# Queries and keys by token tile, turned by DMA transposes, in a fused attention and feed-forward kernel on one core

## The chip, the cores and the metric

The kernel runs on one core of one Trainium2 chip. The metric is the device time of one execution in microseconds (us). The kernel before has a median of 168.66 us over 13 runs, between 167.62 and 169.07.

## The reference

The input x has 2048 tokens of width 448. It is normalised (mean and variance over the width, no gain or bias) to xn. Two branches read xn, and the result joins them. Inputs and output are bf16.

```python
# attention: 16 heads of 28; each token looks back at 8 positions with stride 2
qkv = (xn @ wqkv) -> q, k, v                    # wqkv is 448 x 1344
idx = pos[:, None] - 2 * arange(8)              # masked where negative
attn = softmax(q . k[idx] * 28 ** -0.5)
s = (attn . v[idx]) @ wo                        # wo is 448 x 448
# feed-forward
h = gelu(xn @ w1 + b1)                          # 448 -> 1792, tanh form
g = silu(h @ w2 + b2)                           # 1792 -> 448
out = x + s * g
```

## The kernel before

**Layout.** The tokens are reordered so that all even tokens come first and then all odd ones (`tok`, L188); a stride of two becomes a run of neighbours. There are 16 token tiles of 128 and four chunks of four tiles. The width of 448 is three full contraction tiles of 128 and a rest of 64 rows. The rest is stored twice, in both halves of the partitions, so that two 64-row matmuls can run side by side: the "tails" at L458, L480 and L513. `batch` (L413) puts two outputs' full matmuls first, then a group of tails, and then the full matmuls of two more outputs.

**Stages.** For a token tile, `stats` and `rstds` give mean and 1/deviation, and `norm` (L390) writes xn with tokens on the partitions (L393, L395). It has to be turned so that the width lies on the partitions (`xnT`): by TensorE transposes (L405) for tiles 0 to 7, and by DMA transposes on SyncE (L317) for tiles 8 to 15. `vproj` (L472) makes values with tokens on the partitions: xnT is the stationary operand and 448 columns of weights move. `qk` (L447) makes queries and keys already turned: a group of four heads, each padded from 28 to 32 rows, is the stationary operand (`wqk`, a padded copy of the raw weights `wraw`), and 256 or 512 tokens move. Chunk 0 uses 256 tokens at a time and chunks 1 to 3 use 512. The results are copied into `qT` and `kT`, one tensor for each of four head groups.

`attn` (L570) works on 17 blocks of queries: block 0 has 128 and the others 120, with 128 keys each. For a block, 16 small score products (L580) fill four PSUM banks, ScalarE takes the exponential (L586), VectorE multiplies by a mask (L594), 16 products with values (L602, called PV below) give numerator and denominator, and VectorE divides (L609, L614) into `os`. The 128 keys of a block begin at multiples of 120, so most blocks need values from two token tiles: `values` (L489) assembles them in one of six buffers `v` with two moves within SBUF. In the same way one or two moves put the 120 rows of `os` into token tiles `ot`, and a DMA transpose makes `oT`. All these moves go through `dma_sb` (L309), issued by SyncE.

`ff1` (L504) and `ff2` (L529) are the feed-forward, with GELU on ScalarE; ff2's result goes through y (L552), tanh (L558) and g (L562). `final` (L635) multiplies oT by wo (L639), then by g (L644), adds x (L649) and stores the tile from SyncE (L653).

**What sets the order.** Nothing is issued in source order. Each step is a task with an engine, a cost, dependencies, buffers that it takes and gives, and a priority. `_Plan.run` (L79) plays a list schedule over these costs, and the instructions are then emitted in the order of the planned starts. Each engine, and each queue of DMA issues, keeps that order at run time: an instruction that waits holds all behind it on its engine. The priorities stand in the table `PRIO` (L704). A move on SyncE is charged 0.55 us and a transpose 1.3 us.

```python
def dma_sb(dst, src, deps, take=(), give=()):
    def fn(k):
        nc.sync.dma_start(dst(k), src())
    a = plan.add("SP", 0.55, fn, deps, 75, take=take)
    return a, plan.add("DMA", 0.3, lambda _: None, [a], 75, give=give, tail=1.5)
```

Of the kernel before, what the change touches and what calls it, by code (L numbers as in the profile page):

```python
# [153 lines left out]
def kernel(  # L154
# [39 lines left out]
    def rows(halves, pos, n):  # L194
        h, r = divmod(pos, HALF)
        return halves[h, r:r + n, :]
# [4 lines left out]
    def sb(name, shape, dt=BF16):  # L201
        return const.tile(shape, dt, name=name)
# [13 lines left out]
    b1 = sb("b1", [P, NMT], F32)  # L216
    b2 = sb("b2", [P, D])
    xnT = sb("xnT", [P, KT, S])
    qT = [sb(f"qT{g}", [P, S]) for g in range(G)]
    v_tok = [sb(f"v_tok{t}", [P, H, 32]) for t in range(9)]  # L220
    v_tok = v_tok[8:] + v_tok[1:8] + v_tok[:8]
    kT = [sb(f"kT{g}", [P, S]) for g in range(G)]
    oT = sb("oT", [P, KT, S])
    ident = sb("ident", [P, P])
    eps_t = sb("eps_t", [P, 1], F32)
# [30 lines left out]
    def buf(pool, owner, i=0):  # L256
        return pool.bufs[owner.slots[pool][i]]
# [10 lines left out]
    def copy(e, o, i):  # L268
        if e == "ACT":
            nc.scalar.copy(o, i)  # L270
        else:
            nc.vector.tensor_copy(o, i)
# [33 lines left out]
        a = plan.add(eng, 0.45, fn, [t_on] + list(deps), prio)  # L306
        return plan.add("DMA", kb / (300.0 if prio > 93 else 350.0), lambda _: None, [a], prio, tail=1.7)

    def dma_sb(dst, src, deps, take=(), give=()):  # L309
        def fn(k):  # L310
            nc.sync.dma_start(dst(k), src())
        a = plan.add("SP", 0.55, fn, deps, 75, take=take)
        return a, plan.add("DMA", 0.3, lambda _: None, [a], 75, give=give, tail=1.5)

    def dma_T(dst, src, deps, give):
        def fn(_):
            nc.sync.dma_start_transpose(out=dst, in_=src())  # L317
        a = plan.add("SP", 1.3, fn, deps, 70)
        return plan.add("DMA", 0.6, lambda _: None, [a], 70, give=(give,), tail=1.5)

    t_x = {}

# [67 lines left out]
    def norm(t, prio):  # L390
        def f1(k):
            xn = buf(p_xn, k)
            nc.vector.tensor_scalar(xn[:, :D], x_sb[:, t, :], mv[:, t, 0:1], rstd[:, t:t + 1],  # L393
                                    op0=ALU.subtract, op1=ALU.mult)
            nc.vector.tensor_copy(xn[:, D:], xn[:, KF:D])  # L395

        a = plan.add("DVE", 0.5, f1, [t_rs[t]], prio, take=(p_xn,))
        if t >= 2 * TPC:
            t_xT[t] = dma_T(xnT[:, :, t * P:(t + 1) * P], lambda: buf(p_xn, a)[:], [a], (p_xn, a, 0))
            return  # L400

        def f2(k):
            xn, tp = buf(p_xn, a), half_bank(buf(p_b, k))
            for kt in range(KT):
                nc.tensor.transpose(tp[:, kt, :], xn[:, kt * P:(kt + 1) * P], ident[:])  # L405
        b = plan.add("PE", 0.25, f2, [a, t_ident], prio, take=(p_b,), give=((p_xn, a, 0),), tail=0.15)

        def f3(k):
            copy(k.on, xnT[:, :, t * P:(t + 1) * P], half_bank(buf(p_b, b)))
        t_xT[t] = plan.add(("DVE", "ACT"), (dve(512, 2), act(512)), f3, [b], prio, give=((p_b, b, 0),))  # L410
# [36 lines left out]
    def qk(t0, t1, g, which, prio):  # L447
        cs = slice(t0 * P, t1 * P)
        n = (t1 - t0) * P
        hs = slice(H * which + 4 * g, H * which + 4 * g + 4)  # L450
        r = slice(64 * which, 64 * which + 64)
        dst, done = (kT, t_k) if which else (qT, t_q)

        def full(ps, kt, start, stop):
            nc.tensor.matmul(ps[:, :n], wqk[:, kt, hs, :], xnT[:, kt, cs], start=start, stop=stop)  # L455

        def tail(ps, start, stop):
            nc.tensor.matmul(ps[:, :n], wqk3[r, 4 * g:4 * g + 4, :], xnT[r, 3, cs], start=start, stop=stop)  # L458

        def evac(a, own, i):  # L460
            def fn(k):
                copy(k.on, dst[g][:, cs], buf(p_b, own, i)[:, :n])
            k = plan.add(("ACT", "DVE"), (act(n), dve(n)), fn, [a], prio + 2, give=((p_b, own, i),))
            for t in range(t0, t1):
                done[(g, t)] = k
        return _Job(n, full, tail, which, [t_xT[t] for t in range(t0, t1)] + t_wqk[:3], evac, (), t_wqk[3:])

    t_v, v_at, h_at = {}, {}, {}
    t_vt = {}
# [19 lines left out]
    def values(b):  # L489

        t, r = divmod(BLK[b][2], P)
        if not r:
            t_v[b], v_at[b] = [t_vt[t]], None
            return
        a, d1 = dma_sb(lambda k: buf(p_v, k)[:P - r], lambda: v_tok[t][r:], [t_vt[t]], (p_v,))
        _, d2 = dma_sb(lambda _: buf(p_v, a)[P - r:], lambda: v_tok[t + 1][:r], [a, t_vt[t + 1]])
        t_v[b], v_at[b] = [d1, d2], (p_v, a, 0)
        v_used[t + 8].append(d1)
        v_used[t + 9].append(d2)
# [70 lines left out]
    def attn(b, prio, gate, early):  # L570
# [5 lines left out]
        def f1(k):  # L576
            for g in range(G):
                for hl in range(4):
                    r = slice(32 * hl, 32 * hl + 32)
                    nc.tensor.matmul(buf(p_b, k, hl)[:, g * nq:(g + 1) * nq], kT[g][r, k0:k0 + P],  # L580
                                     qT[g][r, q0:q0 + nq], start=True, stop=True)
        a = plan.add("PE", 0.15, f1, deps + early, prio, take=(p_b,) * 4, tail=0.15, mode=32)
        pv, exps = [], []
        for hl in range(4):
# [35 lines left out]
        while q < q0 + nq:  # L620
            t, row = divmod(q, P)
            n = min(P - row, q0 + nq - q)
            first, d = dma_sb(lambda k, t=t, row=row, n=n: buf(p_ot, ot_at.get(t, k))[row:row + n, :D],
                          lambda q=q, n=n: buf(p_os, o)[q - q0:q - q0 + n, :], [o] + t_os + [d for _, d in ot[t]],
                          () if ot[t] else (p_ot,), ((p_os, o, 0),) if q + n == q0 + nq else ())
            ot[t].append((first, d))
            ot_at[t] = ot[t][0][0]
            if row + n == P:
                t_oT[t] = dma_T(oT[:, :, t * P:(t + 1) * P], lambda t=t: buf(p_ot, ot_at[t])[:], [d for _, d in ot[t]],
                                (p_ot, ot_at[t], 0))  # L630
            q += n
        return exps
# [2 lines left out]
    def final(t, prio):  # L635
        def f1(k):
            ps = buf(p_b, k)
            for kt in range(KT):
                nc.tensor.matmul(ps[:, :D], oT[:, kt, t * P:(t + 1) * P], wo[:, kt, :],  # L639
                                 start=(kt == 0), stop=(kt == KT - 1))  # L640
        a = plan.add("PE", pe(D, KT), f1, [t_oT[t]] + t_wo + [t_f2[min(t + 1, NT - 1)]], prio, take=(p_b,), tail=0.15)

        def f2(k):
            nc.vector.scalar_tensor_tensor(out=buf(p_sg, k)[:], in0=buf(p_b, a)[:, :D], scalar=0.5,  # L644
                                           in1=buf(p_g, t_g[t])[:], op0=ALU.mult, op1=ALU.mult)
        s = plan.add("DVE", dve(D), f2, [a, t_g[t]], prio + 4, take=(p_sg,), give=((p_b, a, 0), (p_g, t_g[t], 0)))

        def f3(k):
            nc.vector.tensor_tensor(out=buf(p_o, k)[:], in0=x_sb[:, t, :], in1=buf(p_sg, s)[:], op=ALU.add)  # L649
        o = plan.add("DVE", dve(D, 2), f3, [s], prio + 4, take=(p_o,), give=((p_sg, s, 0),))  # L650

        def f4(_):
            nc.sync.dma_start(rows(o_half, t * P, P), buf(p_o, o)[:])  # L653
        plan.add("SP", 0.6, f4, [o], 50, give=((p_o, o, 0),), tail=2.0)

    for t in range(2):
        stats(t)
# [27 lines left out]
    for m, w, n, lo, hi in masks:  # L685
# [13 lines left out]
        def fn(_, m=m, w=w, n=n):  # L699
# [1 line left out]
        t_mask.append(plan.add("DVE", 0.3, fn, [t_m, t_st[3]], prio=60))  # L701


    PRIO = {"project": (77, 71, 71, 36.5),  # L704
            "attn": (922.5, 900, 875, 876),
            "ff1": (72.5, 91, 75, 75),
            "ff2": (63, 73, 3, 5),
            "final": (52.5, 36.5, 49.5, 49.5, 93.5, 82.5, 101.5, 48.5)}
    blocks_of = [[b for b, (q0, nq, _) in enumerate(BLK) if (q0 + nq - 1) // CH == c] for c in range(NCH)]
    gate = [early]  # L710

    def project(c):
        p = PRIO["project"][c]
        for t in range(c * TPC, (c + 1) * TPC):
            norm(t, 97 - 2 * t if t < TPC else p + 1)
        vs = [vproj(t, t % 2, p) for t in range(c * TPC, (c + 1) * TPC)]
        if c == 0:
            for i in range(0, len(vs), 2):
                batch(vs[i:i + 1], vs[i + 1:i + 2], 96 if i == 0 else p)
        for t0, t1 in ((0, 2), (2, 4)) if c == 0 else ((c * TPC, (c + 1) * TPC),):  # L720
            for g in (0, 2):
                batch(*[[qk(t0, t1, h, w, p) for w in range(2)] for h in (g, g + 1)], p)
        if c:
            batch(vs[:2], vs[2:], p - 0.1)
        for b in blocks_of[c]:
            values(b)

# [11 lines left out]
    for c, what in ((0, "F"), (0, "A"), (1, "A"), (1, "F"), (2, "A"), (2, "F"), (3, "A"), (3, "F")):  # L739
# [6 lines left out]
        else:  # L746
# [9 lines left out]
                project(2)  # L756
                project(3)
            for t in range(c * TPC, (c + 1) * TPC):
                ff2(t, PRIO["ff2"][c])
    for t in range(NT):  # L760
        final(t, PRIO["final"][t // 2])

    plan.run()
    with tc.manual_schedule():
# [31 lines left out]
```

The softmax here doesn't subtract the row's maximum and nothing guards it: scores larger than these inputs give would overflow.

## Time and profile before

| | |
|---|---|
| median of 13 runs | 168.66 us |
| the profiled run: its own time | 168.19 us |
| the profiled run: span | 166.2 us |
| TensorE busy | 159.0 us |
| ScalarE, VectorE busy | 110.2 and 105.0 us |
| GpSimd busy | 4.4 us |
| DMA issues on SyncE after the loads | 61 moves, 24 transposes, 16 stores |
| granted TensorE clock | 0.993 |

PE is TensorE, PEld its weight loads, DVE VectorE, ACT ScalarE, POOL GpSimd and SP SyncE; SPq is SyncE's queue of instructions. Busy time is a share of the span. A matmul's end is modelled, and neighbours overlap in the pipeline, so the mean of a group is longer than the pace of a run of them. The chain of what ended last lists pieces that follow one another in time, each with its start, its length and its line, so it gives the pace. A group line gives line, engine, operation, output and inputs, shapes, count, then busy time in us and the mean in ns, and then the idle time before the group with what ended it. DMA issues have durations for the issue alone; the transfer comes afterwards.

### The profile page before, as it was taken

What the parts mean: (1) busy time and instruction counts of PE and PEld (TensorE: products, weight loads), DVE (VectorE), ACT (ScalarE), POOL (GpSimd) and SP (SyncE); (2) the same over time, 40 slices, a digit from 0 to 9 for tenths busy, and PEclk for the clock granted to TensorE, in tenths of its full rate; (3) what the DMA queues carried; (4) which work ended last, traced back from release to release, by engine and by line L of the source; (5) the groups of instructions that cost most, each with busy time, mean ns of one, the idle gap of its engine ahead of it and who ended that gap; (6) DMA issues with size and microseconds to landing.
All of it is one profiled execution on the core that took longest, in us unless ns stands there. A gap on an engine that the chain in (4) does not pass through costs nothing.

```text
span 166.2 us, 3522 instructions
## 1 busy us (share of the span) xinstructions
PE 159.0 (96%) x1316; PEld 77.3 (47%) x1328; DVE 105.0 (63%) x278; ACT 110.2 (66%) x201; POOL 4.4 (3%) x29
## 2 busy tenths in 40 slices
PE   6999999999999999999999999999999999999980
PEld 2465535454544355434556533543466553345530
DVE  4798993097899968320296910694798987006672
ACT  3286379987888975698876798455894468851210
POOL 7300000000000000000000000000000000000000
PEclk9999999999999999999999999999999999999997
DMA  5999981034173223234313331022123244100101
GB/s 163 270 392 281 372 286 43 4 62 94 32 93 80 80 76 86 72 90 96 75 37 71 73 82 37 0 83 83 37 70 81 56 130 104 35 0 2 54 30 55
DMA packets 26520, 16.06 MB, mean 97 GB/s; under 512 B 14536, under 2 KB 25992, under 8 KB 26504
## 3 DMA queue, kind: packets, MB, share of 16 engines
q1 hardware_dynamic: 26072, 15.39, 35.1%
q10 hardware_dynamic: 432, 0.46, 0.8%
q8 instruction: 10, 0.16, 0.4%
q14 instruction: 6, 0.05, 0.1%
HBM read 7.06 MB, written 1.84 MB: 53 GB/s over the span
## 4 chain that ended last, share of the span: by engine, by line
PE 93%; DMA 2%; DVE 2%; issue 1%; SPq 0%; DVEq 0%
PE bank L536 25%; PE bank L510 22%; PE bank L455 13%; PE bank L639 7%; PE bank L477 5%; PE bank L513 5%; PE bank L602 4%; PE bank L285 4%; PE bank L580 3%; PE bank L458 3%; DMA v<-v_tok 2%; PE bank L405 1%; PE bank L480 1%; DVE sg L644 1%; DVE o L649 0%
## 5 line engine op out<-in xcount | busy, mean ns | idle before, releaser
L536 PE MATMUL bank<-w,h 128*128 128x448 bf16 x224 | 46.2, 352 | 0.0
L586 ACT ACTIVATE E<-bank 128x480 bf16<-128x480 f32 (+1 forms) x68 | 33.3, 578 | 10.9 <-PE bank L580 10.9
L510 PE MATMUL bank<-xnT,w 128*128 128x512 bf16 x160 | 38.4, 380 | 0.6 <-issue 0.3
L517 ACT ACTIVATE h<-bank,b 128x512 bf16<-128x512 f32 x56 | 34.2, 700 | 4.9 <-PE bank L513 4.8
L536 PEld LDWEIGHTS <-h 128*128 128x128 bf16 x224 | 20.6, 97 | 18.1
L510 PEld LDWEIGHTS <-w 128*128 128x128 bf16 x168 | 15.1, 98 | 21.1 <-issue 5.3
L455 PE MATMUL bank<-xnT,wqk 128*128 128x512 bf16 (+1 forms) x116 | 24.0, 336 | 0.3 <-issue 0.2
L594 DVE TENSOR_TENSOR E<-E,m_gen 128x480 bf16<-128x480 bf16 x60 | 22.3, 403 | 2.5 <-ACT E L586 1.6
L558 ACT ACTIVATE t<-y 128x448 f32<-128x448 f32 x16 | 9.3, 582 | 18.2 <-DVE y L552 18.1
L552 DVE TENSOR_TENSOR y<-bank,b 128x448 f32<-128x448 f32 x16 | 9.8, 619 | 13.5 <-PE bank L536 13.5
L644 DVE SCALAR_TENSOR_TENSOR sg<-bank,g 128x448 bf16<-128x448 f32 x16 | 9.9, 621 | 9.8 <-PE bank L639 9.2
L602 PEld LDWEIGHTS <-E 128*128 128x128 bf16 x272 | 11.4, 96 | 7.9 <-DVE E L594 0.8
L455 PEld LDWEIGHTS <-wqk 128*128 128x128 bf16 x120 | 10.4, 97 | 8.9 <-issue 2.1
L639 PE MATMUL bank<-wo,oT 128*128 128x448 bf16 x64 | 14.1, 352 | 0.1
L270 ACT CAST qT<-bank 128x512 bf16<-128x512 f32 (+1 forms) x17 | 8.5, 499 | 7.2 <-PE bank L458 5.7
L614 DVE TENSOR_TENSOR os<-bank,rd 120x448 bf16<-120x448 f32 (+1 forms) x17 | 10.6, 624 | 3.7 <-DMA ot<-os 3.1
L602 PE MATMUL bank<-v,E 128*128 128x29 bf16 x240 | 11.2, 176 | 0.2 <-DMA v<-v_tok 0.2
L477 PE MATMUL bank<-wv,xnT 128*128 128x448 bf16 x48 | 10.8, 354 | 0.0
L365 DVE BATCH_NORM_STATS2 st<-x_sb 128x6 f32<-128x448 bf16 x16 | 9.6, 603 | 1.3 <-DMA x_sb<-in_A_x_dram 1.3
L562 DVE SCALAR_TENSOR_TENSOR g<-t,y 128x448 bf16<-128x448 f32 x16 | 9.9, 619 | 0.9 <-ACT t L558 0.7
L513 PE MATMUL bank<-xnT,w 64*128 64x512 bf16 x56 | 8.4, 380 | 0.0
L639 PEld LDWEIGHTS <-oT 128*128 128x128 bf16 x64 | 5.9, 97 | 5.2
(60 smaller groups left out, 115.8 us busy)
## 6 DMA issues: line engine op xcount, KB each, us to landing
out_dram<-o SPq DMA_DIRECT2D x16, 112.0 KB
w<-in_B_w_dram SPq DMA_DIRECT2D x1, 1568.0 KB
x_sb<-in_A_x_dram SPq DMA_DIRECT2D x3, 448.0 KB
w<-in_B_w_dram SPq DMA_DIRECT2D x1, 1344.0 KB
wraw<-in_A_wqkv_dram SPq DMA_DIRECT2D x1, 448.0 KB
w<-in_B_w_dram SPq DMA_DIRECT2D x2, 224.0 KB
x_sb<-in_A_x_dram SPq DMA_DIRECT2D x3, 112.0 KB
wo<-in_A_wo_dram SPq DMA_DIRECT2D x1, 336.0 KB
```

The costliest lines, as they stand in the source:

```text
L455: nc.tensor.matmul(ps[:, :n], wqk[:, kt, hs, :], xnT[:, kt, cs], start=start, stop=stop)
L477: nc.tensor.matmul(ps[:, :D], xnT[:, kt, k0:k0 + P], wv[:, kt, :], start=start, stop=stop)
L510: nc.tensor.matmul(ps[:], w1[:, kt, ms], xnT[:, kt, cs], start=start, stop=stop)
L513: nc.tensor.matmul(ps[:], w1[r, 3, ms], xnT[r, 3, cs], start=start, stop=stop)
L517: nc.scalar.activation(buf(p_h, own, i)[:], buf(p_b, own, i)[:], ACT.Gelu_apprx_tanh, bias=b1[:, mt:mt + 1])
L536: nc.tensor.matmul(ps[:, :D], buf(*h_at[(c, mt)])[:, j * P:(j + 1) * P], w2[:, mt, :], start=(mt == 0), stop=(mt == NMT - 1))
L586: nc.scalar.activation(buf(p_E, k)[:, :, :nq], buf(p_b, a, hl)[:, :4 * nq].rearrange("p (g q) -> p g q", g=4), ACT.Exp, scale=SCALE)
L594: nc.vector.tensor_tensor(out=E[:, :, :nq], in0=E[:, :, :nq], in1=m[:, :, :nq], op=ALU.mult)
L602: nc.tensor.matmul(ps[:, h, :DH + 1], buf(p_E, e)[:, g, :], v[:, h, :DH + 1], start=True, stop=True)
L614: nc.vector.tensor_tensor(out=buf(p_os, k)[:nq, :].rearrange("p (h c) -> p h c", h=H), in0=buf(p_b, po)[:nq, :].rearrange("p (h c) -> p h ...
L639: nc.tensor.matmul(ps[:, :D], oT[:, kt, t * P:(t + 1) * P], wo[:, kt, :], start=(kt == 0), stop=(kt == KT - 1))
L644: nc.vector.scalar_tensor_tensor(out=buf(p_sg, k)[:], in0=buf(p_b, a)[:, :D], scalar=0.5, in1=buf(p_g, t_g[t])[:], op0=ALU.mult, op1=ALU.mult)
```

## The change

**Queries and keys.** Chunk 0 stays as it was, apart from the tensors' layout: `qT` and `kT` become one tensor each, with the head group as a middle dimension. For chunks 1 to 3 the new `qk_rows` works on one token tile: xnT is the stationary operand, as for values, and the 448 raw weight columns (`wraw`, `wraw3`) move. The result has tokens on the partitions. It is copied, padded to 32 columns a head, into one of six staging buffers, which are the parts of `wqk` that are no longer needed once chunk 0 is projected. A DMA transpose on SyncE turns each buffer into `qT` or `kT`: 24 new transposes.

**Moves and stores.** The 61 moves within SBUF, and the stores of all token tiles but the last, are issued by GpSimd and not by SyncE. 76 DMAs change queue. SyncE keeps loads, transposes and the last store.

**Order.** DMA priorities now fall with the chunk, the charges are 1.0 us for a move or a store and 1.28 for a transpose, and the priority table is new, with own entries for values, for the second batch of projections in a chunk, for `norm`, and for each tile of ff2 and final. The built program has as many matmuls as before (1328).

```diff
-    qT = [sb(f"qT{g}", [P, S]) for g in range(G)]
+    qT = sb("qT", [P, G, S])
+    kT = sb("kT", [P, G, S])
...
-    def dma_sb(dst, src, deps, take=(), give=()):
+    def dma_sb(dst, src, deps, prio, take=(), give=()):
         def fn(k):
-            nc.sync.dma_start(dst(k), src())
-        a = plan.add("SP", 0.55, fn, deps, 75, take=take)
-        return a, plan.add("DMA", 0.3, lambda _: None, [a], 75, give=give, tail=1.5)
-
-    def dma_T(dst, src, deps, give):
+            nc.gpsimd.dma_start(dst(k), src())
+        a = plan.add("POOL", 1.0, fn, deps, prio, take=take)
+        return a, plan.add("DMA", 0.3, lambda _: None, [a], prio, give=give, tail=2.0)
+
+    def dma_T(dst, src, deps, prio, give):
         def fn(_):
             nc.sync.dma_start_transpose(out=dst, in_=src())
-        a = plan.add("SP", 1.3, fn, deps, 70)
-        return plan.add("DMA", 0.6, lambda _: None, [a], 70, give=(give,), tail=1.5)
+        a = plan.add("SP", 1.28, fn, deps, prio)
+        return plan.add("DMA", 0.6, lambda _: None, [a], prio, give=(give,), tail=1.6)
...
+    p_qk = _Pool([wqk[:, kt, H * w:H * w + H, :] for kt in range(3) for w in range(2)])
+
+    def qk_rows(t, which, prio):
+        cs = slice(t * P, (t + 1) * P)
+        r = slice(64 * which, 64 * which + 64)
+        dst, done = (kT, t_k) if which else (qT, t_q)
+
+        def full(ps, kt, start, stop):
+            nc.tensor.matmul(ps[:, :D], xnT[:, kt, cs], wraw[:, kt, which * D:(which + 1) * D], start=start, stop=stop)
+
+        def tail(ps, start, stop):
+            nc.tensor.matmul(ps[:, :D], xnT[r, 3, cs], wraw3[r, :], start=start, stop=stop)
+
+        def evac(a, own, i):
+            def fn(k):
+                copy(k.on, buf(p_qk, k)[:, :, :DH], buf(p_b, own, i)[:, :D].rearrange("p (h c) -> p h c", h=H))
+            k = plan.add(("ACT", "DVE"), (act(D), dve(D)), fn,
+                         [a] + [d[g, 0] for d in (t_q, t_k) for g in range(G)] + [d[g, 2] for d in (t_q, t_k) for g in range(G)],
+                         prio + 2, take=(p_qk,), give=((p_b, own, i),))
+            m = dma_T(dst[:, :, cs], lambda: buf(p_qk, k).rearrange("p h c -> p (h c)"), [k], 100 - 10 * (t // TPC), (p_qk, k, 0))
+            for g in range(G):
+                done[(g, t)] = m
+        return _Job(D, full, tail, which, [t_xT[t]], evac)
...
-            nc.sync.dma_start(rows(o_half, t * P, P), buf(p_o, o)[:])
-        plan.add("SP", 0.6, f4, [o], 50, give=((p_o, o, 0),), tail=2.0)
+            (nc.sync if t == NT - 1 else nc.gpsimd).dma_start(rows(o_half, t * P, P), buf(p_o, o)[:])
+        plan.add("SP" if t == NT - 1 else "POOL", 1.0, f4, [o], 50, give=((p_o, o, 0),), tail=2.0)
...
-        for t0, t1 in ((0, 2), (2, 4)) if c == 0 else ((c * TPC, (c + 1) * TPC),):
-            for g in (0, 2):
-                batch(*[[qk(t0, t1, h, w, p) for w in range(2)] for h in (g, g + 1)], p)
-        if c:
-            batch(vs[:2], vs[2:], p - 0.1)
+                batch(vs[i:i + 1], vs[i + 1:i + 2], 96 if i == 0 else pv)
+            for t0, t1 in ((0, 2), (2, 4)):
+                for g in (0, 2):
+                    batch(*[[qk(t0, t1, h, w, p) for w in range(2)] for h in (g, g + 1)], p)
+        else:
+            for t, q in ((c * TPC, p), (c * TPC + 2, PRIO["project2"][c])):
+                batch(*[[qk_rows(u, w, q) for w in range(2)] for u in (t, t + 1)], q)
+            batch(vs[:2], vs[2:], pv)
```

## The prediction

> **What bounds the kernel now.** I read the busy shares and the shares of the chain that ended last first.
>
> ```profile
> PE 159.0 (96%) x1316; PEld 77.3 (47%) x1328; DVE 105.0 (63%) x278; ACT 110.2 (66%) x201; POOL 4.4 (3%) x29
> POOL 7300000000000000000000000000000000000000
> PE 93%; DMA 2%; DVE 2%; issue 1%; SPq 0%; DVEq 0%
> ```
>
> TensorE is busy 96% of the span and is 93% of the chain; ScalarE and VectorE have a third of their time free. GpSimd does nothing after the first two of 40 slices. So what counts is PE time taken out, and whether a new wait opens a hole in PE's stream. Next the groups with shapes kept apart, for the projections:
>
> ```profile
> L455 PE MATMUL bank<-xnT,wqk 128*128 128x512 bf16 x68 | 17.2, 379 | 0.3 <-issue 0.2
> L477 PE MATMUL bank<-wv,xnT 128*128 128x448 bf16 x48 | 10.8, 354 | 0.0
> L458 PE MATMUL bank<-xnT,wqk 64*128 64x512 bf16 x24 | 3.6, 381 | 0.0
> L480 PE MATMUL bank<-wv,xnT 64*128 64x448 bf16 x16 | 2.6, 356 | 0.0
> ```
>
> The means overlap in the pipeline, so a price comes from the chain, where pieces follow end to end (start, length, what):
>
> ```profile
> 7.60 0.57 PE bank L477 x3
> ...
> 53.95 0.48 PE bank L480 x4
> ...
> 57.20 4.03 DMA v<-v_tok
> ...
> 107.31 0.65 PE bank L455 x3
> 108.72 0.65 PE bank L455 x3
> 109.36 0.54 PE bank L458 x4
> ...
> 159.87 0.77 PE bank L639 x4
> ...
> 163.01 0.39 DVE o L649
> ```
>
> A 448-column matmul costs 0.57 / 3 = 0.190 us. A 512-column one costs 0.217 here, and 0.225 in the longest runs (2.70 for 12 of L510); four 64-row tails cost 0.54 at 512 and 0.48 at 448. The DMA piece shows that a move of values ended just as the PV product needed it: PE waited only 0.2 us, so the margins are thin. After PE's last matmul, VectorE and one store take 4.8 us to the end. Last, SyncE's timeline and the durations by tile (min/median/max ns, first and last start):
>
> ```profile
> 34.21 5.24 SPq L317 DMA_TRANSPOSE xnT<-xn  x4
> 39.92 0.54 SPq L311 DMA_DIRECT2D ot<-os  x1
> 42.00 1.19 SPq L317 DMA_TRANSPOSE oT<-ot  x1
> ...
> 117.80 5.40 SPq L311 DMA_DIRECT2D v<-v_tok  x7
> ```
>
> ```profile
> L317 SPq DMA_TRANSPOSE oT<-ot x16: 1194/1218/2230, 42.0 to 139.6; - x16
> L311 SPq DMA_DIRECT2D v<-v_tok x30: 511/716/1511, 20.4 to 122.5; - x30
> ```
>
> A SyncE move lands 2.1 us after its issue begins (39.92 to 42.00, where the transpose waited for it). In DMA activity at 0.2 us steps the transposes of 34.21 to 39.45 show bursts of about 0.65 us that begin 1.3 us after each issue; with the move's 0.45 us from last byte to release, a transpose lands about 2.4 us after its issue begins.
>
> **What the Trainium skill says.** "TensorE: Matmul & The Clock Gate", Back-to-back issue gap: warm spacing of about N/2.4 + 2.5 ns, and 131 ns sustained at 512. The trace agrees with the formula for 448 (189 against 190 measured) and not with the 131 (217 to 225 measured), so I price by the trace. "DMA: Bandwidth & Descriptors", Anatomy of one DMA — SWDGE (gpsimd) path: a fixed cost of about 2.0 us plus bytes at 436 GB/s, and in its Latency section a first byte after about 1 us against 0.6 for SyncE's path. No row of before has a GpSimd DMA. The same page, Issuing engines are not separate DMA queues: all queues share 16 engines, so another issuer saves only issue time; the trace has these engines busy some 35% on average, so there is room. "SBUF — State Buffer", Who interferes with whom: VectorE in a two-port mode (copy, tensor_scalar) shuts GpSimd out while it runs. Here those are L393 and L395, 0.39 and 0.18 us; eight pairs (token tiles 8 to 15) fall after the loads.
>
> **The change part by part.** *Query and key projections, token chunks 1 to 3.* Removed: 3 x 24 matmuls of 512 columns and 3 x 8 tails, 72 x 0.2247 + 24 x 0.135 = 19.42 us. Added, with the tokens stationary and the 448 unpadded weight columns moving: 72 x 0.190 + 24 x 0.120 = 16.56. PE saves 2.86 us. The number of weight loads is the same. All of it lies on the path, since PE is the path.
>
> *Evacuations.* 24 copies of 512 become 24 of 448: ScalarE 0.60 to 0.54, VectorE 0.68 to 0.62, some 1.4 us over two engines that are not the bound. I count nothing; if they were exposed it would be a gain of under 1.4.
>
> *24 new transposes on SyncE.* 24 x 1.22 = 29 us of issue and 24 x 0.65 = 16 us of DMA. SyncE loses 61 moves x 0.7 and 15 of its 16 stores x 0.57 to GpSimd, 51 us, so it gets emptier. What matters is order: the transposes of q/k, xn and ot stand in one queue, each behind the waits of those ahead, and a q/k transpose also holds one of six staging buffers that the next evacuations want. If it is late, the copy waits on ScalarE or VectorE, and the exponentials or masks behind it wait too: that is (3) below.
>
> *76 DMAs on GpSimd.* Call c the GpSimd time of one. Below, the nearest row is SyncE's 0.7 us median; above, 1.6, which is the skill's 1 us first byte plus one L393 and one L395 shutting it out. I take 1.0 and landing 2.3 us after that (the skill's 2.0 + 0.26 for 112 KB). Issue alone fits: 76 us in 166. A gain from the move itself is at most the 0.2 us that PE waited for values in before. The 15 stores land later than before (1.0 + 2.3 against 2.1) and hold one of three o buffers so much longer; finals in the built order come at most three together, and the fourth follows 16 us later or at the end, after 4 us, so that is nothing. But the stores also stand between moves in GpSimd's queue, each costing c; they are counted in the strings below.
>
> *Reordered priorities.* The changed kernel can be built, which gives each engine's instructions in order with their waits. I summed PE's order with the prices above (a start of 1.2, warm-up matmuls 0.33, PV products 0.024, score products 0.020): the last matmul ends at 157.1 us before and 154.2 after. Before's real starts run behind that sum, by 2.2 us after the warm-up, 2.4 at 46, 2.9 at 58, 3.5 near 65 and 4.3 at the end; a position in the changed order gets the lag of its stage. Four token tiles of chunk 1 and their first q/k products move ahead of the first feed-forward, which pushes it 2.5 us later. The first GELU waited 2.6 us for its bias copy in before, so ScalarE's late start is covered; xn for tiles 4 to 7 is ready at 16.7 to 19.0, PE asks at 17.0 to 19.0: up to 0.2 us lost.
>
> *New waits, checked one by one in the built order.*
> (1) Final of token tile 1: PE reaches it at 58.5 + 2.9 = 61.4. Its oT transpose needs the eight-row move into ot from block 2, seventh in a string of GpSimd DMAs (one ot, five v, this one) that begins when os of block 1 is ready at 47.8. It lands at 47.8 + 7c + 2.3, plus 2.4 for the transpose: 52.5 + 7c, 59.5 at c = 1. Margin 1.9.
> (2) Final of tile 2, PE at 64.8 + 3.1 = 67.9: five GpSimd DMAs later, 52.5 + 12c, 64.5. Margin 3.4.
> (3) VectorE's copy of a q tile into staging waits for the q transpose of tile 10, which follows that oT and xn's tile 15 on SyncE: issued two transposes (2 x 1.25) later, 55.0 + 7c = 62.0, wanted at 63.3. Behind it on VectorE are the masks of block 5, for which PE waits. Margin 1.3.
> (4) Values of chunk 3: ScalarE ends the GELUs near 114.2, then loads a table (1.28) and runs four exponentials and a tanh (0.58 each) before it copies values (0.54): first copy done at 119.0. Four GpSimd DMAs and a landing follow: 121.3 + 4c = 125.3; PV of block 13 is at 122.1 + 3.5 = 125.6. Margin 0.3. In before these moves began at 117.80 on SyncE.
> q/k tiles themselves are needed 15 to 40 us after they are made (tile 5 made at 22, used at 63), so their transposes' latency is hidden.
>
> At c = 1 nothing is late; I allow 0.3 us for the xn start and thin margin (4). The tail is as before: y, sg, o, g, sg, o, and the last store still on SyncE. The store before it, on GpSimd, lands 1.2 us earlier than the end.
>
> **Sum.** The profiled run took 168.19 (span 166.2 and 2.0 around it), 0.47 under the median. 168.19 - 2.86 + 0.3 = 165.6, so 166.1 against the median of 168.66.
>
> **Rivals.** *A, forecast, 0.60:* 166.1, its own range 165.0 to 167.4.
> *B, SyncE's in-order transposes hold the staging buffers, 0.16.* If transposes issue at their slowest (2.2 us, the maximum above) rather than 1.22, three of them bring (3) to 65.0: VectorE stalls 1.7 us with block 5's masks behind it. 166.1 + 1.7 = 167.8. For it: the chain's 4.03 us move shows DMAs queueing. Against it: the median is 1.22 with few slow ones, and SyncE has lost 76 DMAs.
> *C, GpSimd becomes the bound, slower, 0.20.* From 48 to 78 us some 30 GpSimd DMAs stand in 30 us of PE work. The loss is (12c - 15.4) for (1) and (2) plus (4c - 4.3) for (4): it eats the 2.86 at c = 1.41, and at c = 1.6 it is 3.8 + 2.1 = 5.9, 171.7. For it: a first byte of 1 us in the skill and VectorE's locks. Against it: most moves have 8 to 112 rows, not 128, and the two-port work is small.
> *D, the PE saving isn't real, 0.04:* the tokens as weights cost more, and 168.9 follows. Against it: L477 already works that way, at 0.190.
>
> **The numbers.** About 0.3% (0.5 us) is what can be told from no change. Faster: all of A and half of B, 0.68. Same: 0.06 of B and 0.02 of D, 0.08. Slower: C and the rest, 0.24. The range reaches from 164.8 (margins all hold and the evacuations help a little) to 170.2, which takes in the bound of c up to about 1.5 and leaves out 0.12 of C above and 0.04 below.
>
> **What would show it.** Right: the q/k group has 448 columns and 72 + 24 matmuls, 0.57 a three; PE still over 95% of a span near 163.6; GpSimd DMAs of about 1.0 us; VectorE waits on transposes under 1 us. Wrong: PE idle before L602 or the oT products on a DMA (C), VectorE idle before the staging copies (B), 0.65 for three q/k matmuls (D).

## The result and the profile after

The changed kernel takes 170.59 us (median of 11 runs, 170.34 to 172.64), against 168.51 for the kernel before in 48 runs that include those taken beside it. The ratio is 1.016, with a 95% interval of 1.0135 to 1.0187; it follows the means, and four of the 11 runs, at 171.65 to 172.64, pull the mean up. By the medians the kernel is slower by 2.1 us. 166.1 was predicted, with a range of 164.8 to 170.2.

The profiled run took 170.62 us, of which the span is 168.9 (before: 168.19 and 166.2). From the summary of its profile come first the busy times, then two rows in 40 slices of 4.2 us (busy tenths), then the chain's shares by engine:

```profile
PE 157.0 (93%) x1320; PEld 76.4 (45%) x1328; DVE 102.0 (60%) x273; ACT 112.1 (66%) x206; POOL 45.4 (27%) x105
...
PE   7999999999999979999999999999999999999900
...
DMA  5899999004589996586530114510032254100120
...
PE 83%; DMA 6%; SPq 3%; DVE 2%; issue 1%; ACT 1%; DVEq 0%
```

TensorE is busy 2.0 us less than before in the records, so its work did shrink. But its share of the chain fell from 93% to 83%, and two places in its row are new: a 7 in the 15th slice (59 to 63 us), and two empty slices at the end where there was one. The DMA row is at 9 in that slice and the two before it. The mean granted clock is lower than before, 0.982 against 0.993, but that isn't the cause: up to 158 us it is 1.00 in both kernels, and it falls only at the end, where TensorE has nothing more to do. The groups with shapes kept apart:

```profile
L312 POOL DMA_DIRECT2D ot<-os x31 | 16.5, 536 | 58.1 <-DVE os L640 32.6 <-DVE xn L394 25.4
L478 PE MATMUL bank<-wraw,xnT 128*128 128x448 bf16 x72 | 16.4, 353 | 0.0
L679 POOL DMA_DIRECT2D out_dram<-o x15 | 8.4, 557 | 25.2 <-DVE o L675 23.5 <-DVE rd L635 1.7
L481 PE MATMUL bank<-wraw,xnT 64*128 64x448 bf16 x24 | 3.3, 354 | 0.0
```

The 96 query and key matmuls are there, with no idle time before any of them, and a GpSimd DMA issue takes 0.54 to 0.56 us, not 1.0.

**The hole near 62 us.** The chain of the changed kernel from 54 to 64 us (start, length, what):

```profile
54.62 1.26 SPq L318
55.88 0.05 issue
55.93 1.26 SPq L318
57.19 0.04 issue
57.23 1.27 SPq L318
...
58.67 4.94 DMA oT<-ot
63.62 0.05 issue
63.66 0.93 PE bank L665 x4
```

and TensorE's timeline there (in brackets the idle time before an entry, and what ended it):

```profile
61.36 0.74 PE L478 MATMUL bank<-wraw,xnT 128*128 128x448 bf16 x3
63.66 0.93 PE L665 MATMUL bank<-wo,oT 128*128 128x448 bf16 x4 [1.56 <-DMA oT<-ot]
```

PE reaches the final of token tile 1 near 62.1 and waits 1.56 us for its oT. Ahead of that transpose on SyncE stand three xn transposes, issued back to back. It is issued at 58.67 and lands 4.94 us later, the longest landing of the 16 oT transposes of this run:

```profile
DMA to landing us min/median/max: 2.4/2.8/4.9
```

**The end.** Shown are the last operations in the changed kernel's timeline, and GpSimd's closing instructions in the changed kernel and in the kernel before (min/median/max ns, first and last start us). The longest DRAIN, below called the Drain, is the first that GpSimd runs after it has handed over its last DMA; semaphore instructions follow it, and then the program ends.

```profile
161.29 0.54 POOL L679 DMA_DIRECT2D out_dram<-o  x1 [1.16 <-DVE o L675]
...
162.29 0.39 DVE L675 TENSOR_TENSOR o<-x_sb,sg 128x448 bf16<-128x448 bf16 x1
162.71 0.37 SPq L679 DMA_DIRECT2D out_dram<-o  x1
```

```profile
L822 POOLq EVENT_SEMAPHORE  x4: 17/17/17, 168.2 to 168.8; - x4
L822 POOLq DRAIN  x3: 40/106/6842, 161.3 to 168.6; - x3
```

```profile
L791 POOLq EVENT_SEMAPHORE  x4: 17/17/17, 165.6 to 166.1; - x4
L791 POOLq DRAIN  x3: 34/82/331, 5.4 to 166.0; - x3
```

VectorE ends at 162.68, 0.72 us earlier than before (163.40), but the span ends 6.2 us after that and not 2.8. In between nothing computes. GpSimd's first Drain begins at 161.3, when its last store is handed over, lasts 6.84 us, and its semaphore instructions follow at 168.2. Before, the longest Drain was 0.33.

So the span's account is: VectorE ends 0.72 earlier, where 2.86 was expected, and the end takes 3.4 longer: 166.2 - 0.7 + 3.4 = 168.9.

### The profile page after: what moved, and what is told of

The parts are those of the page before. It is cut to its first block, busy times and chain, and to the rows that moved or that the text cites. A ratio compares the mean times of both kernels' runs of the same rounds, so it can differ in the third digit from the quotient of the medians.

```text
span 168.9 us, 3596 instructions
## 1 busy us (share of the span) xinstructions
PE 157.0 (93%) x1320; PEld 76.4 (45%) x1328; DVE 102.0 (60%) x273; ACT 112.1 (66%) x206; POOL 45.4 (27%) x105
## 3 DMA queue, kind: packets, MB, share of 16 engines
q0 software_dynamic: 3072, 5.53, 13.6%
## 4 chain that ended last, share of the span: by engine, by line
PE 83%; DMA 6%; SPq 3%; DVE 2%; issue 1%; ACT 1%; DVEq 0%
PE bank L562 25%; PE bank L536 22%; PE bank L478 7%; PE bank L665 6%; PE bank L503 5%; PE bank L539 4%; PE bank L628 4%; PE bank L456 3%; PE bank L606 3%; DMA oT<-ot 3%; DMA wraw<-in_A_wqkv_dram 3%; SPq L318 2%; SPq L305 1%; PE bank L481 1%; PE bank L506 1%; PE bank L406 1%
## 5 line engine op out<-in xcount | busy, mean ns | idle before, releaser
L543 ACT ACTIVATE h<-bank,b 128x512 bf16<-128x512 f32 x56 | 34.7, 688 | 10.6 <-PE bank L539 6.7
L312 POOL DMA_DIRECT2D ot<-os x31 | 16.5, 536 | 58.1 <-DVE os L640 32.6
L312 POOL DMA_DIRECT2D v<-v_tok x30 | 16.2, 543 | 31.9 <-ACT v_tok L270 14.7
L478 PE MATMUL bank<-wraw,xnT 128*128 128x448 bf16 x72 | 16.4, 353 | 0.0
L679 POOL DMA_DIRECT2D out_dram<-o x15 | 8.4, 557 | 25.2 <-DVE o L675 23.5
L270 ACT CAST wqk<-bank 128x448 bf16<-128x448 f32 x17 | 8.5, 550 | 4.7 <-PE bank L478 2.9
```

The source lines that it names most:

```text
L312: nc.gpsimd.dma_start(dst(k), src())
L478: nc.tensor.matmul(ps[:, :D], xnT[:, kt, cs], wraw[:, kt, which * D:(which + 1) * D], start=start, stop=stop)
L543: nc.scalar.activation(buf(p_h, own, i)[:], buf(p_b, own, i)[:], ACT.Gelu_apprx_tanh, bias=b1[:, mt:mt + 1])
```

## The experiments

**Theories.** Theory 1: PE's saving is real; it is lost to two new costs, the wait for the oT of tile 1 and a later end that comes with any use of GpSimd's DMAs. Rivals: the late end comes from the late stores or from the number of GpSimd DMAs (2); it comes from the transposes or the new order (3); all of the loss comes from the new order and the transposes (4). For the wait there were two candidates: the order of SyncE's queue, and DMA engines crowded by GpSimd's moves. Ratios and medians are compared with runs of the kernel before on the same chip (168.4 in each set).

### Which DMAs bring the late end

*One move by GpSimd*, in the kernel before:

```diff
+    moved = []
...
-            nc.sync.dma_start(dst(k), src())
+            (nc.sync if moved else nc.gpsimd).dma_start(dst(k), src())
+            moved.append(k)
```

> The kernel before, with one of its 61 moves (the first, of values, near 20 us) issued by GpSimd; all else as it was. Theory 1 (a program that has any GpSimd DMA ends later by a fixed 3.4 us): from VectorE's last operation to the end of the span 6.2 us in place of 2.8, PE's last matmul where it was (161.4), about 171.9 us. Rival 2 (the late end comes from the stores that GpSimd issues close to the end, or grows with the number of its DMAs): the end stays at 2.8 to 3.0 and the time at 168.5.

Measured: 168.38 us, ratio 1.001 (0.9988 to 1.0028). Theory 1 fell in that form: a single early GpSimd DMA costs nothing. Its Drain:

```profile
L794 POOLq DRAIN  x3: 34/102/6628, 10.2 to 166.2; - x3
```

It lasted 6.6 us here too, from 10.2 us on, beside the input loads, where this move took 6.5 us to land. Nobody waited for it. So the Drain lasted here until the DMA before it had landed, and its length alone is no cost; its end can be.

*Stores by SyncE*, in the changed kernel, the moves still by GpSimd:

```diff
-            (nc.sync if t == NT - 1 else nc.gpsimd).dma_start(rows(o_half, t * P, P), buf(p_o, o)[:])
+            nc.sync.dma_start(rows(o_half, t * P, P), buf(p_o, o)[:])
```

> The changed kernel with its 15 early stores issued by SyncE again, the 61 moves still by GpSimd (the last of them 40 us before the end); the order of every other engine is unchanged. Theory 1: the end stays at 6.2 us after VectorE's last operation, 170.6 us, or 0.2 to 0.3 less if a store no longer takes DMA time from the transpose that PE waits for. Rival 2, late stores: the end shrinks to 2.8 and the time to 167.2. Rival 2, number: the end shrinks by a fifth, to about 5.5.

Measured: 167.32 us, ratio 0.993 (0.9905 to 0.9946), the end 2.7 us after VectorE's last operation. The last GpSimd DMA is a move at 138.8, its Drain of 6.1 us is over by 145, and the late end is gone. PE's wait of 1.6 us for the oT stays. This version already beats the kernel before.

*All moves and stores by SyncE*, in the changed kernel:

```diff
-            nc.gpsimd.dma_start(dst(k), src())
+            nc.sync.dma_start(dst(k), src())
...
-            (nc.sync if t == NT - 1 else nc.gpsimd).dma_start(rows(o_half, t * P, P), buf(p_o, o)[:])
+            nc.sync.dma_start(rows(o_half, t * P, P), buf(p_o, o)[:])
```

> The changed kernel with all moves and stores issued by SyncE, in the order that was planned for two queues; no GpSimd DMA is left. Theory 1: the end is 2.8 us after VectorE's last operation; but SyncE, which was nearly solid from 41 to 84 us with transposes alone, gets some 30 moves of 0.7 more there, so PE's wait for the first oT transposes grows from 1.6 us to 5 or more: 168 to 173 us, with PE's last matmul at 163 or later. Rival 3 (the late end comes from the transposes or the new order, not from GpSimd's DMAs): the end stays at 6.2.

Measured: 181.04 us, ratio 1.073 (1.067 to 1.0785). The end is 2.8 us again, so rival 3 fell. SyncE's queue costs more than I had expected (168 to 173 us); the longest waits for DMAs on PE's side, those of its weight loads, are now (engine and line, what it waited for: us in total, times, longest):

```profile
PEld L478 <- DMA xnT<-xn: 6.1, 1, 6.1
...
PEld L665 <- DMA oT<-ot: 4.5, 2, 3.1
```

In SyncE's queue transposes and moves now stand behind one another, in an order that was planned for two queues. With 24 more transposes on SyncE, this order of work needs the moves on another queue.

*All 61 moves and 15 stores by GpSimd*, in the kernel before, queries and keys and all charges as they were:

```diff
-            nc.sync.dma_start(dst(k), src())
+            nc.gpsimd.dma_start(dst(k), src())
...
-            nc.sync.dma_start(rows(o_half, t * P, P), buf(p_o, o)[:])
+            (nc.sync if t == NT - 1 else nc.gpsimd).dma_start(rows(o_half, t * P, P), buf(p_o, o)[:])
```

> The kernel before with all 61 moves and 15 stores issued by GpSimd, queries and keys as they were, each engine's order unchanged. Theory 1: 0.54 us of GpSimd for each, PE's last matmul at 161.4 or up to 0.3 earlier, the end 6.2 us after VectorE's last operation, 171.6 to 171.9 us. Rival 2 (number): the same end as the changed kernel, so it is told apart by the run with one move. Rival 4 (the loss comes from the new order and the transposes alone): 168.5.

Measured: 172.6 us, ratio 1.025 (1.018 to 1.032). The end is 5.9 us after VectorE's last operation, with a Drain of 6.842 us, to the ns that of the changed kernel. Rival 4 fell. The profiled run was the slowest of its four (173.88): its first GELUs waited for an input load, so its middle isn't read.

*Only the 61 moves by GpSimd*, in the kernel before:

```diff
-            nc.sync.dma_start(dst(k), src())
+            nc.gpsimd.dma_start(dst(k), src())
```

> The kernel before with its 61 moves by GpSimd and all 16 stores by SyncE; queries and keys as before. It splits the run with all of both on GpSimd (172.6 us) into the moves and the late stores. If the late end of 3.1 us is all that the stores cost, and the moves cost nothing: 168.4. If the moves lose time by themselves (later landing, DMA engines): 169.0 to 169.5.

Measured: 168.27 us, ratio 1.000 (0.998 to 1.0024). The moves are neutral by themselves. So the stores account for the loss of the run before it: 4.3 us by the medians, of which the traces show 3.2 as the end (5.9 against 2.7). The rest isn't explained; with four runs, the interval of that ratio is some 2.3 us wide.

### Late, or many?

*One late store by GpSimd*, in the kernel before, no other GpSimd DMA:

```diff
-            nc.sync.dma_start(rows(o_half, t * P, P), buf(p_o, o)[:])
+            (nc.gpsimd if t == NT - 2 else nc.sync).dma_start(rows(o_half, t * P, P), buf(p_o, o)[:])
```

> The kernel before with one store by GpSimd, that of token tile 14, issued near 161.8 us; every move and the other 15 stores stay on SyncE. In the changed kernel and in the one with all moves and stores on GpSimd the span ends 7.1 us after the end of GpSimd's last DMA issue (161.83 to 168.9; 165.12 to 172.2). Theory 1 in its new form (GpSimd needs some 7 us after its last DMA before the program can end, however few there are): span 169.4, time 171.5. Rival (it is the number of stores that counts): 168.4 to 168.7.

Measured: 168.41 us, ratio 1.000 (0.998 to 1.0024), no loss. The new form (some 7 us after the last one, however few) fell as well: the Drain took 2.2.

```profile
L791 POOLq DRAIN  x3: 34/89/2215, 162.3 to 166.4; - x3
```

*The last five stores by SyncE*, in the changed kernel:

```diff
-            (nc.sync if t == NT - 1 else nc.gpsimd).dma_start(rows(o_half, t * P, P), buf(p_o, o)[:])
+            (nc.sync if k in stores[-5:] else nc.gpsimd).dma_start(rows(o_half, t * P, P), buf(p_o, o)[:])
...
     plan.run()
+    stores.sort(key=lambda a: a.start)
```

> The changed kernel with the last five stores by SyncE (all after 157 us); the 11 earlier ones stay on GpSimd, the last of them near 140.7 us. Theory 1 in its new form: GpSimd would be done by 148.4, nothing is left of the late end: 2.8 us after VectorE's last operation, 167.1 to 167.4 us, as with all stores on SyncE. Rival (number): with 11 of 15 stores and all moves left on GpSimd most of the 3.4 us stays, 169.5 to 170.6.

Measured: 167.44 us, ratio 0.993 (0.9895 to 0.996). With 72 DMAs still on GpSimd the Drain takes 6.6 us, but from 141.3: it is hidden. A large number alone doesn't cost anything either.

*Four late stores by GpSimd*, in the kernel before (first diff), and *one late store after 61 moves*, in the changed kernel (second diff). `stores` holds the tasks of all 16 stores, sorted by their planned start as above:

```diff
-            nc.sync.dma_start(rows(o_half, t * P, P), buf(p_o, o)[:])
+            (nc.gpsimd if k in stores[-5:-1] else nc.sync).dma_start(rows(o_half, t * P, P), buf(p_o, o)[:])
...
```

```diff
-            (nc.sync if t == NT - 1 else nc.gpsimd).dma_start(rows(o_half, t * P, P), buf(p_o, o)[:])
+            (nc.gpsimd if k is stores[-2] else nc.sync).dma_start(rows(o_half, t * P, P), buf(p_o, o)[:])
...
```

> The kernel before with four stores by GpSimd, the four next to the last one (issued between 155 and 162.4 us); no other GpSimd DMA. GpSimd's closing Drain took 6.8 us after 76 DMAs with four late stores (the changed kernel) and 2.2 us after a single one. If the Drain grows with the few DMAs just before it: 5 to 6.8 us from 162.9, span 168.3 to 169.9, time 170.3 to 171.9. If it grows with all the GpSimd DMAs of a program: 2.2 to 2.5 us as with one, time 168.4.

> The changed kernel with one store by GpSimd, that of 161.3 us, and the other 15 by SyncE; the 61 moves stay on GpSimd, the last of them near 139 us, so this is one late DMA after 61 early ones. If the Drain grows with the DMAs just before it: 2.2 us as with one alone, hidden, time 167.3. If it grows with all of a program: 6 to 6.8 us from 161.9 to 162.5, span 168.5 to 169.4, time 170.2 to 171.

Measured: 167.91 us (ratio 0.997, 0.9936 to 1.0004) for four late ones, and 169.79 (1.009, 1.007 to 1.012) for a single late one after 61 early ones, a little under the 170.2 that was expected. Of the profile with four late stores, the slowest run of twelve (169.84), only the end is read. The Drains, in this order:

```profile
L794 POOLq DRAIN  x3: 34/102/2195, 164.1 to 167.9; - x3
```

```profile
L825 POOLq DRAIN  x3: 40/106/5736, 160.9 to 167.2; - x3
```

It takes both: many GpSimd DMAs in the program, and one of them late. The last of the 61 moves had been issued 22 us before this Drain began, and it still took 5.7.

*15 stores*, and *30 moves of values and one late store*, by GpSimd in the kernel before (first and second diff, with `stores` as above):

```diff
-            nc.sync.dma_start(rows(o_half, t * P, P), buf(p_o, o)[:])
+            (nc.gpsimd if k is not stores[-1] else nc.sync).dma_start(rows(o_half, t * P, P), buf(p_o, o)[:])
...
```

```diff
-            nc.sync.dma_start(dst(k), src())
+            (nc.gpsimd if src().shape[-1] == 32 else nc.sync).dma_start(dst(k), src())
...
-            nc.sync.dma_start(rows(o_half, t * P, P), buf(p_o, o)[:])
+            (nc.gpsimd if k is stores[-2] else nc.sync).dma_start(rows(o_half, t * P, P), buf(p_o, o)[:])
...
```

> The kernel before with the 15 earlier stores by GpSimd (1920 rows of 896 bytes) and all moves by SyncE: 15 GpSimd DMAs, the last near 162.4 us. The closing Drain was 2.2 us after 1 and after 4 GpSimd DMAs, 5.7 after 62 and 6.8 after 76. If it grows with their number, some 0.06 to 0.08 us each: 2.9 to 3.3 us, span 166.5 to 167, time 168.4 to 168.8. If it grows with the rows they carry: about the same as the run with 31 DMAs beside this one, near 3.5.

> The kernel before with the 30 moves of values (15 pairs, together 1920 rows of 1 KB) and the store of token tile 14 by GpSimd: 31 GpSimd DMAs, 2048 rows, the last near 162.4 us. If the Drain grows with the number of DMAs: 3.8 to 4.3 us from 163.0, span 167.6, time 169.3 to 169.7. If with the rows: as the run with 15 stores, near 3.5, time 169. If it is a step (long only above some number): 2.2 or 5.7, 168.4 or 171.

Measured: 168.47 and 167.94 us, ratios 0.999 and 0.9985 with intervals that contain 1. The Drains are 2.65 and 3.35 us, both shorter than expected. All the late ones together:

| GpSimd DMAs in the program | packets on its queue | Drain, us | time, us |
|---|---|---|---|
| 1 | 48 | 2.2 | 168.41 |
| 4 | 192 | 2.2 | 167.91 |
| 15 | 720 | 2.65 | 168.47 |
| 31 | 1232 | 3.35 | 167.94 |
| 62 | 2400 | 5.74 | 169.79 (changed order) |
| 76 | 3072 | 6.84 | 170.59 (changed order) |

The new order isn't what makes the last two Drains long: the kernel before with all 76 on GpSimd had the same 6.842. The hidden Drains fit in, 5.6 to 6.1 us after the 61 moves and 6.6 after 72 DMAs. So the Drain is long after many GpSimd DMAs whether the last is late or not; a late one is what exposes it.

It is no step at a fixed number between 31 and 76: from 31 to 62 and from 62 to 76 it rises by 0.077 and 0.079 us for each DMA, from 15 to 31 by 0.044. After 1 and 4 it is about as long as such a store takes to land (1.9 to 2.1 us). Rows alone don't set it, since 1920 and 2048 rows gave 2.65 and 3.35. Number and packets aren't told apart.

### The wait for the oT of token tile 1

All three kernels start from the one with all stores on SyncE (167.32 us) and change the order of emission on one queue after the planning.

*oT one place ahead on SyncE:*

```diff
     plan.run()
+    late = [a for t in (14,) for a in (t_xT[t].deps[0], t_xT[t])]
+    plan.order = [a for a in plan.order if a not in late]
+    i = plan.order.index(t_oT[1].deps[0]) + 1
+    plan.order[i:i] = late
```

> The changed kernel with all stores on SyncE, and on SyncE's queue the oT transpose of token tile 1 one place ahead, before the xn transpose of tile 14; no other engine's order changes. Its eight-row move lands near 57.8 to 58.3, it was issued at 58.7 to 59.1. If the order of the queue makes PE's wait of 1.6 us: issue 0.9 us earlier and one transpose less in flight, landing near 61, wait under 0.5 us, 166.0 to 166.4 us. If the crowded DMA engines make it (landing 4.9 us after issue where 2.4 is usual): 0.9 us less of wait at most, 166.5 to 167.0. If neither: 167.3.

Measured: 165.62 us, ratio 0.986 (0.982 to 0.991), the lowest median here (two of its six runs took 166.7 and 167.4) and faster than both kernels. Its chain:

```profile
56.91 0.05 issue
...
57.08 4.87 DMA oT<-ot
61.95 0.05 issue
62.00 0.93 PE bank L665 x4
```

The transpose is issued 1.6 us earlier than in the changed kernel and takes about as long to land. PE's wait for it is gone from the list of waits; a weight load still waits 0.6 us, where it was 2.0. So an earlier place in SyncE's queue is enough to end the wait. It gained more than the 0.9 I had expected, as the eight-row move landed near 56.8, sooner than I had read.

*Values of blocks 7 to 9 later on GpSimd's queue:*

```diff
     plan.run()
+    late = [a for d in t_v[7] + t_v[8] + t_v[9][:1] for a in (d.deps[0], d)]
+    plan.order = [a for a in plan.order if a not in late]
+    i = plan.order.index(t_v[9][1].deps[0])
+    plan.order[i:i] = late
```

> The changed kernel with all stores on SyncE, and on GpSimd's queue five moves of values for blocks 7, 8 and 9 that are needed only after 76 us put behind the moves of 54 to 61 us; SyncE's order is unchanged, its transposes as many. If the crowded DMA engines make PE's wait: the oT transpose of tile 1 lands 2.4 to 3.5 us after issue in place of 4.9 to 5.1, and the wait goes: 165.7 to 166.2 us. If SyncE's queue makes it: the transpose is issued at 59 still and the wait stays over 1 us, 167.0 to 167.3.

Measured: 167.31 us, and a landing of 5.07. This told nothing: GpSimd issued the postponed moves from 58.3 to 61.7, in the flight of the very transpose (58.43 to 63.50). The next kernel puts all six moves behind those of block 10:

```diff
-    late = [a for d in t_v[7] + t_v[8] + t_v[9][:1] for a in (d.deps[0], d)]
+    late = [a for d in t_v[7] + t_v[8] + t_v[9] for a in (d.deps[0], d)]
...
-    i = plan.order.index(t_v[9][1].deps[0])
+    i = plan.order.index(t_v[10][1].deps[0]) + 1
```

> The changed kernel with all stores on SyncE, and on GpSimd's queue six moves of values (blocks 7 to 9) put behind the values of block 10, which GpSimd can only issue near 65.5 us. In the run before this one they had landed in the very flight of the oT transpose of tile 1, so nothing was told. If the crowded DMA engines make PE's wait: that transpose lands 2.4 to 3.5 us after issue in place of 5, the wait of 1.5 us goes, 165.6 to 166.2 us, if the later moves bring no wait of their own. If the transposes ahead of it are enough to make it late: landing 4.5 to 5 us after issue and the wait stays, 167.3.

Measured: 166.29 us, ratio 0.986 (0.982 to 0.990). Its chain:

```profile
57.53 1.27 SPq L318
...
58.98 3.83 DMA oT<-ot
62.81 0.05 issue
62.85 0.93 PE bank L665 x4
```

With GpSimd's queue at 2% of the DMA engines' time during the flight the same transpose lands in 3.83 us, and PE's wait falls from 1.6 to 0.9. In the kernel that this one starts from, the landing was 5.06, with GpSimd's queue at 18%; in the changed kernel it was 4.94 at 48%. So moves beside it cost 1.1 to 1.2 us, but not in proportion to their share. That is between my two expectations: 1.4 us over the 2.4 of the prediction remain with hardly anything but transposes in flight. The wait has two causes, and each of the two remedies alone gains 1 to 1.7 us by the medians.

## Why the prediction was wrong

**Right in kind, a fifth too large: PE's saving.** The new matmuls run at the pace that was forecast for them, three in 0.57 to 0.58 us in most pieces of the chain, so rival D is out:

```profile
64.59 0.57 PE bank L478 x3
```

With wait and late end taken away (oT ahead), the last matmul ends at 159.00, 2.38 us before that of the kernel before, where 2.86 was predicted. The sum had priced the two sides unlike: the old matmuls at 0.2247, the pace in long runs, the new ones at 0.190, the shortest pace. The prediction's own lines have three of L455 in 0.65, 0.217 each. An estimate from 0.217 and 0.190 gives 72 x 0.027 + 24 x 0.015 = 2.3 us.

**Right: margins (2), (3), (4), the evacuations, the stores' o buffers.** The list of waits of the changed kernel has neither PE nor VectorE waiting for a later oT, a q/k transpose or values.

**Wrong in the safe direction: c.** I took 1.0 us within 0.7 to 1.6; it is 0.54, below my lower bound, the issue row of SyncE. So rival C, the way to a slower result that I had priced at 171.7, didn't happen. The sign given for it, PE idle before the oT products on a DMA, did appear, but not from GpSimd's string of issues. That the measured time lies near C's number is luck.

**Failed: margin (1), 1.9 us.** The step was "It lands at 47.8 + 7c + 2.3, plus 2.4 for the transpose". Its first part, the move landed at 57.1, came out nearly right by luck. At the true c the string would have been issued by 51.6; but the eight-row move waited for block 2's os and was issued at 54.39, close to the 53.8 that c = 1 had given. It landed near 57.8. What failed is "plus 2.4 for the transpose", which took SyncE and the DMA engines to be free. There is no term for SyncE's queue: with three xn transposes ahead, this one was issued at 58.67. And its landing was 4.94, not 2.4. So oT came at 63.6 and not at 59.5; PE came 0.7 later than the forecast 61.4, and margin (1) became a wait of 1.6 us.

That SyncE "gets emptier" came from sums over the whole run (in which 0.57 us for a store is the longest issue; the median is 0.33). In its timeline from 41 to 66 us its issues fill the window in the changed kernel, where they filled some 22 of 25 us before. Eleven of the 24 new transposes fall there, where the moves left. The DMA engines in the same window, in the kernel before and in the changed one (packets, MB, share of the 16 engines; q1 is SyncE's queue, q0 GpSimd's):

```profile
q1 hardware_dynamic: 4242, 1.91, 36.6%
```

```profile
q1 hardware_dynamic: 10016, 2.42, 52.7%
q0 software_dynamic: 736, 1.31, 31.1%
```

Rival B named SyncE's in-order transposes, but made them late by slow issues (2.2 us; the three ahead of the hole took 1.26 to 1.27) and at the staging buffers. That its price of 1.7 us is near the wait of 1.6 is luck too.

The Trainium skill, "DMA: Bandwidth & Descriptors", Issuing engines are not separate DMA queues, which the prediction cites, says that all queues share 16 engines. I set an average of 35% against it. That holds for the kernel before, in this window too (37%); the change itself brings it to 84%. The landing of 3.83 against 5.06 with the moves beside it agrees with the page and shows what the sharing costs.

**Failed: the tail, priced at nothing.** The step was "The tail is as before ... The store before it, on GpSimd, lands 1.2 us earlier than the end." What was late is not this store, issued at 161.29, but the engine that issued it. I had priced when the data of the moved stores arrive, and not what else the program's end waits for: GpSimd itself, whose longest Drain was 0.33 us before and is now 6.84. No row of before shows such a Drain, and a new engine's part in the end should have been bounded from both sides like c. The same page's Anatomy of one DMA — SWDGE (gpsimd) path gives about 2.0 us of fixed cost for a single DMA. The traces agree for such late stores (1.9 to 2.1 us to land in the kernels with 1, 4 and 31 of these DMAs), but that is no price for the Drain. This term alone, 3.4 us, turns the forecast's gain into the loss: without it the kernel takes 167.32 us, and without the wait as well 165.62.

**The sum with the measured terms.** -2.3 for PE's work (the estimate above), +1.6 for the wait at the oT, +3.4 at the end: +2.7 for the span, as measured (168.9 - 166.2). The medians differ by 2.1, since the profiled run of the kernel before was 0.3 under its median and its time lies 2.0 us over its span, that of the changed kernel 1.7.

**Left open.** What GpSimd does in the Drain, and whether its length goes by DMAs or by packets. That moves in flight delay a transpose was shown for this one transpose alone, and that the transposes ahead of it account for the remaining 1.4 us was not tested.

## What to carry to other kernels

When DMAs move to another engine, follow that engine to the end of the program too: the Drain after 61 or 72 DMAs on GpSimd was hidden here when the last was issued over 20 us before the end, and one more in the last 7 us cost 2.4 us, so leave the last stores to another queue. Judge a queue and the DMA engines in the stretch where the step falls, with the load that the change itself puts there; price a DMA transpose by its place in the queue and by what flies beside it; and take both prices of a difference at the same kind of pace.

## What the runs showed of the hardware

- GpSimd's closing Drain, in kernels that moved 1 to 76 of these DMAs, took 2.2 us after 1 or 4 of them issued late, 5.6 to 6.1 after 61, 5.7 after 62, 6.6 after 72 and 6.8 after 76, though most of these had been issued long before. A single one beside the input loads took 6.5 us to land, and its Drain 6.6.
- In the changed kernel a GpSimd DMA issue took 0.54 us for a move and 0.56 for a store, where SyncE's medians before were 0.7 and 0.33. Its landing took 1.6 to 7.0 us.
- A DMA transpose into oT took 1.2 us to issue. Its landing took 2.4 us at the least, 2.8 in the median of the changed kernel, and for tile 1 3.8 with hardly anything but transposes in flight and 4.9 to 5.1 with moves within SBUF beside them.
